# Loading a second weight matrix with converting DMAs issued from GpSimd

## The chip, the cores and the metric

The kernel runs on one core of one Trainium2 chip. The metric is the device time of one execution in microseconds (us), several executions per kernel. TensorE (PE) multiplies (PEld are its weight loads); VectorE (DVE), ScalarE (ACT) and GpSimd (POOL) work elementwise; SyncE (SP) issues DMAs here. The profile books all DMAs, whoever issues them, on the core's 16 DMA engines.

## The reference

Blockwise linear attention, then a two-layer network with SiLU on its output:

```python
# q, k, v: (4, 8, 768, 64) f32
for b in range(nb):                                # blocks of 64 positions
    intra = (q_b @ k_b.T * decay_mask) @ v_b
    inter = (q_b * lam_pow) @ kv_state
    out_b = intra + inter
    kv_state = lam_block * kv_state + (k_b * rev_pow).T @ v_b
x = out as (3072 tokens, 512)
h = x @ w_in                                       # (512, 2048)
g = h * sigmoid(h)
y = g @ w_out                                      # (2048, 512), f32 out
```

w_in and w_out are 4.2 MB each in f32. The kernel multiplies in bf16.

## The kernel before

The tokens go in 24 chunks of 128; the first four form group 0, which runs attention, the up-projection (w_in), then the down-projection (w_out), while the weights still arrive. Both weight matrices come in eight pieces of 512 KB. SP loads each piece as f32 into one of eight buffers; DVE (here and there ACT) casts it to bf16 in its place.

```python
W_IN = [((0, 2), (0, 512)), ((2, 4), (0, 512)), ((0, 4), (512, 768)), ((0, 4), (768, 1024)),
        ((0, 2), (1024, 1536)), ((2, 4), (1024, 1536)), ((0, 2), (1536, 2048)), ((2, 4), (1536, 2048))]
# a row of a piece is 2 KB in DRAM, but 1 KB in pieces 2 and 3

def load_w(which, *pieces):
    for i in pieces:
        src = w_piece(which, i, ...)
        t = wio.tile([128, 1024], F32, name="w_tmp", tag="w_tmp", bufs=WBUFS)      # WBUFS = 8
        ...
        nc.sync.dma_start(out=t, in_=src)
        wtmp[which, i] = t

def cast_w(which, i, e="D"):                       # e: D = DVE, A = ACT
    dst, t = w_piece(...), wtmp.pop((which, i))
    ...                                            # copy t to dst, f32 -> bf16

load_q(0), load_k(0), ..., load_v(3)               # group 0, on the SP queue
load_w("in", *range(8))
load_w("out", *range(6))
load_q(4)
load_k(4), load_k(5)
load_w("out", 6, 7)
load_v(4), load_v(5)
...                                                # the attention of group 0, in the order of ORDER:
#   ... vc:3,D (cast v of chunk 3 on DVE) ... x:1,A ... w:0,DA z:1,o d:3 o:3,att f:0,0 x:3,A w:1,DA kv:3,A f:0,1 ... w:2,D w:3,D
clear_halves(2, 3)                                 # POOL memsets
...
for i in range(4, 8):
    cast_w("in", i)
for m in range(4, 16):
    ffn1(0, m)                                     # up-projection, 4 matmuls of 128x512 each
for i in range(6):
    cast_w("out", i)
down0(0, 2, 3, 0, 1)                               # down-projection: needs w_out pieces 0 and 1
...
```

Of the kernel before, what the change touches and what calls it, by code (L numbers as in the profile page):

```python
# [24 lines left out]
ORDER = """  # L25
# [9 lines left out]
def kernel(  # L35
# [10 lines left out]
    nc = tc.nc  # L46
# [38 lines left out]
        out=ident, in_=ident, compare_op=AL.not_equal, fill=1.0,  # L85
# [5 lines left out]
        out=mask, in_=mask, compare_op=AL.is_ge, fill=0.0,  # L91
# [44 lines left out]
    w_out_bf = wpool.tile([128, KO_OUT, DM], BF16)  # L136
# [7 lines left out]
    def w_piece(which, i, src, dst):  # L144
        (k0, k1), (a, z) = W_IN[i] if which == "in" else ((2 * i, 2 * i + 2), (0, DM))
        return (src if dst is None else dst)[:, k0:k1, a:z]

    def load_w(which, *pieces):
        for i in pieces:
            src = w_piece(which, i, w_in_r if which == "in" else w_out_r, None)  # L150
            t = wio.tile([128, 1024], F32, name="w_tmp", tag="w_tmp", bufs=WBUFS)
            t = t.rearrange("p (ko f) -> p ko f", ko=src.shape[1])
            nc.sync.dma_start(out=t, in_=src)  # L153
            wtmp[which, i] = t

    def move(e, dst, src):
        if e == "A":
            nc.scalar.activation(dst, src, AF.Copy)  # L158
        else:
            nc.vector.tensor_copy(dst, src)  # L160

    def cast_w(which, i, e="D"):

        dst, t = w_piece(which, i, None, w_in_bf if which == "in" else w_out_bf), wtmp.pop((which, i))
        n = dst.shape[1] // len(e)
        for h, x in enumerate(e):
            move(x, dst[:, n * h:n * h + n, :], t[:, n * h:n * h + n, :])
# [27 lines left out]
    def load_q(c):  # L195

        b, blk = divmod(c, NB)
        sl = slice(blk * BLK, (blk + 2) * BLK)
        qf = io.tile([128, H, 2, D], F32, name="qf2", tag="qf2", bufs=2)
        nc.sync.dma_start(out=qf.rearrange("p h r d -> p h (r d)"),  # L200
                          in_=q[b, :, sl, :].rearrange("h (p r) d -> p h (r d)", r=2))
        rawq[c] = qf
# [9 lines left out]
    def load_k(c):  # L212
        rawk[c] = load_1(k, c, "kf", 6)

    def load_v(c):
        vraw[c] = load_1(v, c, "vf", 6)
# [253 lines left out]

    load_q(0), load_k(0), load_k(1), load_q(2), load_k(2), load_v(0), load_k(3), load_v(1), load_v(2), load_v(3)
    load_w("in", *range(8))
    load_w("out", *range(6))
    load_q(4)
    load_k(4), load_k(5)
    load_w("out", 6, 7)
    load_v(4), load_v(5)
    load_c(6)
    load_c(7)
# [20 lines left out]
    def op_z(n, tag="kv"):  # L500
# [8 lines left out]
        "s": keep("s", pe_s), "m": op_m, "d": pe_d, "kv": copy_kv, "o": keep("o", pe_o),  # L509
        "x": lambda c, e: move(e, xt[0][:, :, c * BLK:(c + 1) * BLK], cell["o", c]),  # L510
        "w": lambda i, e: cast_w("in", i, e), "f": op_f, "z": op_z,
    }
    for word in ORDER.split():
        name, _, args = word.partition(":")
        table[name](*[int(a) if a.isdigit() else a for a in args.split(",")])

# [19 lines left out]
# [3 lines that stand above are left out]
        ffn1(0, m)  # L539
    for i in range(6):  # L540
        cast_w("out", i)
# [110 lines left out]
```

## Time and profile before

| | before |
|---|---|
| median of 3 runs | 220.1 us (219.55 to 220.37) |
| span of the profiled run | 218.3 us |
| PE busy | 207.6 us |
| start of group 0's up-projection, second half | 22.48 us |
| start of group 0's down-projection | 35.89 us |

The page of the kernel before: busy time of each engine, with its share of the span and its instructions.

```profile
PE 207.6 (95%) x1642; PEld 129.7 (59%) x1642; DVE 109.8 (50%) x257; ACT 103.9 (48%) x216; POOL 59.7 (27%) x68
```

PE is busy 95% of the span and everything else about half. A change gains or loses only where it moves one of PE's waits, or PE's clock.

The timeline of PE before, in the stretch in question. A line starts with the start and the time taken; in brackets stand PE's idle time before it and what ended it.

```profile
20.18 1.05 PE L419 MATMUL h_ps<-xt,w_in_bf 128*128 128x256 bf16 x8
22.48 13.58 PE L419 MATMUL h_ps<-xt,w_in_bf 128*128 128x256 bf16 x72 [1.25 <-DVE w_in_bf L160]
35.89 7.07 PE L445 MATMUL o_ps<-w_out_bf,g 128*128 128x512 bf16 x32
```

After one wait of 1.25 us for the second w_in piece, PE runs without a break from 22.48 us through the up-projection into the down-projection.

The timeline of DVE before: the cast of the fourth v piece (vpad), then those of the w_in pieces. The bracket of a cast tells that DVE waited for the piece to land.

```profile
18.14 0.42 DVE L160 CAST vpad<-vf 128x512 bf16<-128x512 f32 x1
...
26.20 0.69 DVE L160 CAST w_in_bf<-w_tmp 128x1024 bf16<-128x1024 f32 x1 [0.67 <-DMA w_tmp<-in_moe_w_in_dram]
27.56 0.69 DVE L160 CAST w_in_bf<-w_tmp 128x1024 bf16<-128x1024 f32 x1 [0.66 <-DMA w_tmp<-in_moe_w_in_dram]
28.90 0.69 DVE L160 CAST w_in_bf<-w_tmp 128x1024 bf16<-128x1024 f32 x1 [0.65 <-DMA w_tmp<-in_moe_w_in_dram]
30.27 0.69 DVE L160 CAST w_in_bf<-w_tmp 128x1024 bf16<-128x1024 f32 x1 [0.67 <-DMA w_tmp<-in_moe_w_in_dram]
```

These are pieces 4 to 7. One lands every 1.36 us, which is 385 GB/s: the DMA engines are full (their busy share is 1.04 to 1.05 in every 2 us from 24 to 36 us). Piece 5 serves the last 30 matmuls of the up-projection and piece 7 the last 14. At 0.86 us per four, counted back from 35.89 us, PE needs them at 29.4 and 32.9 us; their casts end at 28.25 (27.56 and 0.69) and 30.96, so the slack is about 1.2 and 1.9 us.

### The profile page before, as it was taken

To read this page: it belongs to the slowest core of one execution; us is meant where nothing else is said; L and a number is where in the kernel's file an instruction comes from. 1 tells how busy PE (TensorE), PEld (TensorE's weight loads), DVE (VectorE), ACT (ScalarE), POOL (GpSimd) and SP (SyncE) were. 2 spreads that over 40 slices of the span, in tenths; PEclk is the share of its full clock that TensorE was granted. 3 is DMA by queue.
4 is the path that set the end of the run, shared out by engine and by line. 5 is a ranking of instruction groups with operands and counts; after the bars stand their busy time and mean duration, and the time that the engine had idled before them with its cause. 6 is when DMAs were issued, how large, how long until landed. Compare 5 with 4: busy or idle time off the path is not lost.

```text
span 218.3 us, 4252 instructions
## 1 busy us (share of the span) xinstructions
PE 207.6 (95%) x1642; PEld 129.7 (59%) x1642; DVE 109.8 (50%) x257; ACT 103.9 (48%) x216; POOL 59.7 (27%) x68
## 2 busy tenths in 40 slices
PE   7778899999899999999989999999999999999994
PEld 2356544456776877766646566556555555566654
DVE  7796455177594668646744553835671333001121
ACT  4776765052662665554554445444444443443310
POOL 7565100616941432333313233433000000000000
PEclk9999999999999999999999999999999999999999
DMA  4999999999997999999999979999610111011112
GB/s 120 243 217 349 378 387 349 248 235 219 237 249 156 200 214 142 228 142 230 216 153 209 204 142 205 223 226 228 128 50 0 48 51 47 2 51 50 48 48 99
DMA packets 97941, 38.04 MB, mean 174 GB/s; under 512 B 86912, under 2 KB 91392, under 8 KB 97920
## 3 DMA queue, kind: packets, MB, share of 16 engines
q1 hardware_dynamic: 97776, 37.76, 80.8%
q8 instruction: 13, 0.21, 0.4%
q14 instruction: 8, 0.07, 0.2%
q10 hardware_dynamic: 144, 0.00, 0.0%
HBM read 27.27 MB, written 6.29 MB: 154 GB/s over the span
## 4 chain that ended last, share of the span: by engine, by line
PE 47%; DMA 30%; SPq 14%; POOL 5%; issue 1%; DVE 1%; POOLq 0%
PE o_ps L445 22%; PE h_ps L419 19%; DMA qf<-in_q_dram 16%; SPq L209 8%; DMA w_tmp<-in_moe_w_in_dram 5%; DMA w_tmp<-in_moe_w_out_dram 5%; POOL qb L245 4%; SPq L263 3%; DMA kn<-kb 2%; PE op L396 2%; SPq L153 2%; DMA kf<-in_k_dram 2%; PE o_part L459 2%; PE sp L365 1%; POOL kb L239 1%
## 5 line engine op out<-in xcount | busy, mean ns | idle before, releaser
L423 ACT ACTIVATE g<-h_ps 128x256 bf16<-128x256 f32 (+2 forms) x144 | 64.8, 455 | 79.9 <-PE h_ps L419 78.6
L419 PE MATMUL h_ps<-xt,w_in_bf 128*128 128x256 bf16 (+2 forms) x592 | 100.1, 304 | 1.8 <-DVE w_in_bf L160 1.3
L445 PE MATMUL o_ps<-w_out_bf,g 128*128 128x512 bf16 x368 | 92.3, 379 | 0.3 <-DVE w_out_bf L160 0.3
L419 PEld LDWEIGHTS <-w_in_bf 128*128 128x128 bf16 x592 | 55.4, 98 | 33.6 <-DVE w_in_bf L160 1.8
L445 PEld LDWEIGHTS <-g 128*128 128x128 bf16 x368 | 34.9, 98 | 30.5 <-issue 0.5
L449 DVE COPY ob<-o_ps 128x512 f32<-128x512 f32 x23 | 15.9, 692 | 43.5 <-PE o_ps L445 43.4
L245 POOL TENSOR_TENSOR qb<-qf,lam_fwd 128x512 bf16<-128x512 f32 x18 | 18.8, 1043 | 63.9 <-DMA qf<-in_q_dram 63.9
L372 DVE TENSOR_TENSOR ss<-sp,mask 128x512 bf16<-128x512 f32 (+1 forms) x48 | 26.2, 585 | 18.1 <-PE sp L365 16.8
L239 POOL TENSOR_TENSOR kb<-kf,lam_bwd 128x512 bf16<-128x512 f32 x23 | 24.3, 1059 | 5.8 <-DMA kf<-in_k_dram 4.9
L276 DVE COPY vpad<-vb 64x256 bf16<-64x256 bf16 x72 | 18.3, 254 | 1.6
L160 DVE CAST kvbd<-kv_ps 64x256 bf16<-64x256 f32 x32 | 13.5, 421 | 9.0 <-PE kv_ps L341 8.8
L404 ACT ACTIVATE xt<-op 128x512 bf16<-128x512 f32 x20 | 11.9, 597 | 9.2 <-PE op L396 8.6
L160 DVE COPY ktbd<-kn 64x512 bf16<-64x512 bf16 x32 | 10.8, 339 | 10.7 <-DMA kn<-kb 10.4
L365 PEld LDWEIGHTS <-ktbd 128*128 128x128 bf16 x192 | 11.2, 98 | 6.9 <-DVE ktbd L160 3.9
L365 PE MATMUL sp<-qt,ktbd 128*128 128x128 bf16 (+1 forms) x192 | 13.4, 210 | 2.0 <-DVE ktbd L160 1.8
L396 PE MATMUL op<-ss,vpad 128*128 128x128 bf16 (+1 forms) x192 | 12.7, 209 | 0.0
L158 ACT ACTIVATE vb<-vf 128x512 bf16<-128x512 f32 x18 | 11.2, 622 | 0.0
L396 PEld LDWEIGHTS <-vpad 128*128 128x128 bf16 x192 | 10.9, 98 | 0.3
L234 POOL TENSOR_TENSOR qb<-qf,lam_fwd 128x512 bf16<-128x512 f32 x4 | 4.6, 1166 | 20.1 <-DMA qf<-in_q_dram 18.5
L504 PE MATMUL warm_ps<-kvbd 128*128 128x512 bf16 x26 | 8.5, 453 | 1.3 <-DVE kvbd L104 1.3
L160 DVE CAST w_in_bf<-w_tmp 128x1024 bf16<-128x1024 f32 (+1 forms) x8 | 5.2, 644 | 6.1 <-DMA w_tmp<-in_moe_w_in_dram 6.1
L341 PEld LDWEIGHTS <-kb 128*128 128x128 bf16 x80 | 6.1, 98 | 3.3 <-issue 0.9
(63 smaller groups left out, 95.4 us busy)
## 6 DMA issues: line engine op xcount, KB each, us to landing
kf<-in_k_dram SPq DMA_DIRECT2D x24, 256.0 KB, 4.8
vf<-in_v_dram SPq DMA_DIRECT2D x24, 256.0 KB, 5.0
out_dram<-ob SPq DMA_DIRECT2D x23, 256.0 KB, 3.7
qf<-in_q_dram SPq DMA_DIRECT2D x18, 256.0 KB, 3.9
w_tmp<-in_moe_w_in_dram SPq DMA_DIRECT2D x8, 512.0 KB, 9.3
w_tmp<-in_moe_w_out_dram SPq DMA_DIRECT2D x8, 512.0 KB, 10.0
qf<-in_q_dram SPq DMA_DIRECT2D x3, 512.0 KB, 5.9
qt<-qb SPq DMA_TRANSPOSE x16, 3.9
```

The lines of the kernel that those rows point to most:

```text
L160: nc.vector.tensor_copy(dst, src)
L209: nc.sync.dma_start(out=t, in_=src[b, :, blk * BLK:(blk + 1) * BLK, :].rearrange("h s d -> s h d"))
L239: VG[e].tensor_tensor(kb, rawk.pop(c).rearrange("s (p j) d -> s p j d", j=2), decay(lam_bwd, c % NB), op=AL.mult)
L245: nc.gpsimd.tensor_tensor(qb, rawq.pop(c).rearrange("s (p j) d -> s p j d", j=2), decay(lam_fwd, c % NB), op=AL.mult)
L276: nc.vector.tensor_copy(vh[64 * j:64 * j + 64, :, h, j, :], vb[64 * h:64 * h + 64, :, j, :])
L365: nc.tensor.matmul(sp[:, p, :], lhsT=lhsT, rhs=qt[:, p, a:], start=True, stop=True)
L372: VG[e].tensor_tensor(ss, sp, m[:, None, :n].to_broadcast([128, 4, n]), op=AL.mult)
L396: nc.tensor.matmul(dst, lhsT=lhsT, rhs=rhs, start=(i == 0), stop=(i >= len(terms) - NP), skip_group_check=True)
L419: nc.tensor.matmul(hp[:, a:z], lhsT=w_in_bf[:, ko, m * 128:(m + 1) * 128], rhs=xt[g][:, ko, a:z], start=(ko == 0 and a == 0), stop=(ko == ...
L423: nc.scalar.activation(gg, hp[:, :n], AF.Silu)
L445: nc.tensor.matmul(o, lhsT=gt[g, ko][:, mt * BLK:(mt + 1) * BLK], rhs=w_out_bf[:, ko, :], start=(ko == 0), stop=(ko == KO_OUT - 1))
L449: nc.vector.tensor_copy(ob, o)
```

## The change

The intent: spare DVE and ACT the w_out casts and SP the w_out issues, by letting DMAs convert on the way. They are issued from GpSimd.

```diff
     def load_w(which, *pieces):
         for i in pieces:
             src = ...
+            if which == "out":
+                nc.gpsimd.dma_start(out=w_piece(which, i, None, w_out_bf), in_=src)
+                continue
 ...
     def cast_w(which, i, e="D"):
+        if which == "out":
+            return
 ...
     load_w("in", *range(8))
-    load_w("out", *range(6))
     load_q(4)
     load_k(4), load_k(5)
-    load_w("out", 6, 7)
 ...
-    for word in ORDER.split():
+    words = ORDER.split()
+    for i, word in enumerate(words):
+        if word == "x:1,A":
+            load_w("out", *range(8))
```

## The prediction

The sum came to 225.5 us (the terms as written add up to 225.6).

> **What bounds the kernel now.** TensorE. The page's busy table gives PE 207.6 of 218.3 us, at full granted clock. By the table of stretches PE is idle 2.6 us in 0-10, 1.4 us in 10-20 and 1.4 us in 20-30; from 30 us on it idles about 2.5 us in all, before the tail. Four matmuls of 128x512 follow each other every 0.86 us (the chain of waits), so they run back to back. DVE is 50% busy, ACT 48%, POOL 27%: what they do costs nothing unless PE waits for it.
>
> **Where the weights are tight.** From 17 to 36 us the DMA engines are full (share about 1.05, 380 to 390 GB/s). All loads are on the one SP queue, in order: w_in, then w_out. In the timeline of DVE the w_in pieces land one per 1.36 us (512 KB): casts start at 23.36, 24.84, 26.20, 27.56, 28.90, 30.27. PE needs them nearly at once: counting 0.86 us per up-projection tile from 22.48 us, the tiles of pieces 4 and 5 start at about 28.5 (last cast ends 28.25) and those of 6 and 7 at about 32.0 (last cast ends 30.96). Slack is 0.3 and 1.0 us. The w_out pieces land with more room (pieces 0 and 1 cast by 33.7, used at 35.9; only a 0.34 us PE wait at 48.5).
>
> **What the change does.** Removes seven DVE casts (0.69 us each) and one ACT cast (1.06 us), all in PE's shadow: worth about 0.3 us. Removes 9.3 us of SP issue, so q, k, v of chunks 4 to 7 are requested earlier: no PE wait worth more than about 1 us hangs on those. Adds eight issues on POOL; behind the last prepared k (ends 15.06 us) nothing holds them, so they start there, not at 21 to 40 us as before. POOL's next urgent work is at 40 us, so issuing may cost it 10 to 20 us unpunished.
>
> **The cost.** The 4 MB of w_out now travel beside w_in instead of after it. [...] At half of 385 GB/s a w_in piece takes 2.7 us instead of 1.36. From about 17 us the last one then lands near 38 (estimate: 8.4 MB at 385 GB/s from 16.5 us) instead of 30.3; its tiles start at about 39 instead of 32. PE loses about 7 us in several waits, mostly before 40 us, and nothing later gives them back. If the cast makes the transfers slower, [...] the loss is 10 us or more[...]. [...]
>
> Sum: 220.1 + 6.5 lost to late w_in - 1 from the gaps that go = 225.5 us. Faster by over 2% would need 4.4 us, more than PE idles after 22.5 us.
>
> **What would show it.** A second, software DMA queue of 4.2 MB read; PE waits on w_in casts between 21 and 40 us of 4 to 8 us in sum; w_in's issue-to-landing median up from 9.3 to 13 us or more; total PE busy about unchanged; PE idle after 45 us at or under before's.
>
> **What would make it wrong.** The software queue gets a small share beside the hardware queue, yet w_out is still on time: then 219 to 221. Or POOL starts the issues later than 15 us. Or cast transfers are far slower than plain ones, or PE's clock falls in the waits: then over 232.

## The result, and the profile after

The changed kernel takes 226.47 us (median of 4 runs, 225.63 to 226.9), against 219.82 us for the kernel before on the same chip. The ratio is 1.029, with a 95% interval of 1.026 to 1.032: slower. All ratios here are the mean time of one kernel's fast runs over that of the other's in the same rounds, so not quite the ratio of the medians. A run counts as slow when it is over 1.5% above the fastest of the same kernel; all runs named are fast unless it is said otherwise. The granted clock is the share of its full clock that TensorE was given, by the profile; 1.00 is full.

The page after, busy time and then DMA queues (packets, MB, share of 16 engines' span):

```profile
PE 209.8 (94%) x1642; PEld 131.2 (59%) x1642; DVE 112.0 (50%) x250; ACT 102.4 (46%) x215; POOL 66.3 (30%) x76
...
q1 hardware_dynamic: 95600, 33.57, 72.1%
q0 software_dynamic: 2176, 2.10, 5.5%
```

The new software queue q0 carries w_out. Its MB are those written as bf16; it reads twice as many.

The timeline of PE after:

```profile
21.23 0.40 PE L346 MATMUL kv_ps<-vpad,kb 128*128 128x128 bf16 x4 [2.18 <-DVE vpad L163]
...
24.18 10.10 PE L424 MATMUL h_ps<-xt,w_in_bf 128*128 128x256 bf16 x50 [1.50 <-DVE w_in_bf L163]
34.99 3.63 PE L424 MATMUL h_ps<-xt,w_in_bf 128*128 128x512 bf16 x16 [0.72 <-DVE w_in_bf L163]
40.45 3.19 PE L424 MATMUL h_ps<-xt,w_in_bf 128*128 128x512 bf16 x14 [1.83 <-DVE w_in_bf L163]
43.48 7.07 PE L450 MATMUL o_ps<-w_out_bf,g 128*128 128x512 bf16 x32
```

Four waits stand where there was one, and the down-projection starts 7.6 us later (43.48 against 35.89). The first two do not wait for late data: the v cast and the first w_in cast, whose data had landed, ended late on DVE. Only 0.72 and 1.83 us are waits for late pieces. The four waits sum to 6.2 us, 5.0 more than before; the other 2.6 us of the delay are, by subtraction, PE at a lower clock (below). The span grew by 5.5 us (223.8 against 218.3), so 2.1 us came back afterwards: from the start of the down-projection on, PE waits 0.6 us in all by the list of waits (2.2 before).

The timeline of DVE after, same casts:

```profile
18.22 2.95 DVE L163 CAST vpad<-vf 128x512 bf16<-128x512 f32 x1
...
31.48 0.69 DVE L163 CAST w_in_bf<-w_tmp 128x1024 bf16<-128x1024 f32 x1 [2.00 <-DMA w_tmp<-in_moe_w_in_dram]
34.24 0.69 DVE L163 CAST w_in_bf<-w_tmp 128x1024 bf16<-128x1024 f32 x1 [2.07 <-DMA w_tmp<-in_moe_w_in_dram]
36.93 0.69 DVE L163 CAST w_in_bf<-w_tmp 128x1024 bf16<-128x1024 f32 x1 [2.00 <-DMA w_tmp<-in_moe_w_in_dram]
39.70 0.69 DVE L163 CAST w_in_bf<-w_tmp 128x1024 bf16<-128x1024 f32 x1 [2.08 <-DMA w_tmp<-in_moe_w_in_dram]
```

Two things are to be seen. The w_in pieces now land 2.7 us apart, twice as far as before, and the last is cast 9.4 us later. And the v cast, the same instruction as before, took 2.95 us instead of 0.42. The timeline of POOL says what it met:

```profile
15.01 5.91 POOL L152 DMA_DIRECT2D w_out_bf<-in_moe_w_out_dram  x8
```

POOL is busy with the eight issues, a median of 0.74 us each, from 15.01 to 20.92 us; DVE's cast ends at 21.17. (The theories below call this descriptor writing; the profile shows the issues and their time, not what they write.) The first w_in cast on DVE was long too, 1.84 us from 22.28 us instead of 0.45. It ran beside two POOL memsets, from 22.00 to 23.83 us, that came later than before because POOL was busy; no run separates this from the issues themselves. The third new thing is in the table of stretches (start and end, then length, busy time of PE, PEld, DVE, ACT, POOL with counts, granted clock, DMA share, GB/s):

```profile
22.00:24.00 2.00, 0.67 (x7) 0.40 (x4) 2.00 (x2) 1.29 (x3) 2.00 (x4) 0.50 1.18 247
24.00:26.00 2.00, 1.82 (x9) 1.33 (x10) 1.97 (x3) 0.46 (x2) 1.94 (x3) 0.50 1.16 247
26.00:28.00 2.00, 2.00 (x12) 1.38 (x11) 0.00 (x0) 0.00 (x0) 0.12 (x1) 0.50 1.18 266
```

PE's granted clock is halved (0.50) from about 22 to 28 us; before it was full throughout (1.00).

### The profile page after: what moved, and what is told of

It reads as the page before. It is cut to its first block, busy times and chain, and to the rows that moved or that the text cites. A ratio compares the mean times of both kernels' runs of the same rounds, so it can differ in the third digit from the quotient of the medians.

```text
span 223.8 us, 4245 instructions
## 1 busy us (share of the span) xinstructions
PE 209.8 (94%) x1642; PEld 131.2 (59%) x1642; DVE 112.0 (50%) x250; ACT 102.4 (46%) x215; POOL 66.3 (30%) x76
## 3 DMA queue, kind: packets, MB, share of 16 engines
q0 software_dynamic: 2176, 2.10, 5.5%
## 4 chain that ended last, share of the span: by engine, by line
PE 69%; ACT 1%; DVE 0%; issue 0%
PE o_ps L450 29%; PE h_ps L424 29%; PE op L401 4%; PE sp L370 3%; PE o_part L464 2%; PE kv_ps L346 1%; ACT xt L409 1%; ACT g L428 0%; DVE ktbd L163 0%; DVE ob L163 0%; PE tp L330 0%; PE tp L328 0%
## 5 line engine op out<-in xcount | busy, mean ns | idle before, releaser
L424 PE MATMUL h_ps<-xt,w_in_bf 128*128 128x256 bf16 (+2 forms) x592 | 102.4, 309 | 4.6 <-DVE w_in_bf L163 4.1
L424 PEld LDWEIGHTS <-w_in_bf 128*128 128x128 bf16 x592 | 56.4, 100 | 37.7 <-DVE w_in_bf L163 5.3
L281 DVE COPY vpad<-vb 64x256 bf16<-64x256 bf16 x72 | 20.6, 286 | 1.6
L409 ACT ACTIVATE xt<-op 128x512 bf16<-128x512 f32 x20 | 11.9, 597 | 11.3 <-PE op L401 10.7
L163 DVE CAST w_in_bf<-w_tmp 128x1024 bf16<-128x1024 f32 (+1 forms) x8 | 7.2, 914 | 11.0 <-DMA w_tmp<-in_moe_w_in_dram 11.0
L163 DVE COPY ktbd<-tk 64x512 bf16<-64x512 bf16 x10 | 4.2, 421 | 12.8 <-PE tk L318 12.3
## 6 DMA issues: line engine op xcount, KB each, us to landing
w_tmp<-in_moe_w_in_dram SPq DMA_DIRECT2D x8, 512.0 KB, 13.7
```

The costliest lines, as they stand in the source:

```text
L163: nc.vector.tensor_copy(dst, src)
L281: nc.vector.tensor_copy(vh[64 * j:64 * j + 64, :, h, j, :], vb[64 * h:64 * h + 64, :, j, :])
L409: nc.scalar.activation(xt[g][:, :, off * BLK:(off + 1) * BLK], op, AF.Copy)
L424: nc.tensor.matmul(hp[:, a:z], lhsT=w_in_bf[:, ko, m * 128:(m + 1) * 128], rhs=xt[g][:, ko, a:z], start=(ko == 0 and a == 0), stop=(ko == ...
```

## The experiments

Two theories were set against each other. A: w_out shares the DMA engines with w_in, and late w_in pieces set the pace. B: writing descriptors on POOL, that is, issuing the DMAs there, blocks DVE's casts, PE waits, and its clock falls. Both were seen in the trace (pieces 2.7 us apart; a cast of 2.95 us and a clock of 0.50); the question was which of them the 6 us are.

| kernel | last w_in cast starts | down-projection starts | median, us | ratio to before (95%) |
|---|---|---|---|---|
| before | 30.27 | 35.89 | 219.82 | 1 |
| the change | 39.70 | 43.48 | 226.47 | 1.029 (1.026 to 1.032) |
| e1: after w_in | 29.51 | 36.84 | 222.43 | 1.011 (1.007 to 1.015) |
| e2: descriptors only | 31.45 | 39.63 | 223.45 | 1.014 (1.011 to 1.018) |
| e3: traffic only | 39.32 | 43.10 | 225.24 | 1.024 (1.020 to 1.028) |
| e4: casts on ACT | 40.92 | 44.71 | 227.00 | 1.032 (1.028 to 1.036) |
| f4: half early | 35.46 | 39.99 | 222.66 | 1.018 (1.013 to 1.023) |
| f6: waits filled | 40.90 | 44.68 | 226.59 | 1.035 (1.031 to 1.039) |
| f3: half late | 29.76 | 35.63 | 219.90 | 1.004 (1.001 to 1.008) |
| f7: quarter late | 29.57 | 35.48 | 221.25 | 1.011 (1.006 to 1.016) |
| f9: half rows | 36.07 | 39.85 | 225.28 (the two fast: 222.69) | none (two of four runs slow) |
| f10: half later | 30.00 | 35.69 | 220.20 | 1.001 (0.995 to 1.007) |

In the five rows where the last w_in cast starts after 36 us (the change, e3, e4, f6, f9), the down-projection starts 3.78 us after it each time, to within 0.01 us: 0.69 us of cast, then the last tiles. There nothing but that piece sets the time. In the kernel before it is 5.62 us: the piece is early by 1.84 us. The change casts it 9.43 us later; less those 1.84 us this is 7.59 us, just what the down-projection lost.

All gave the right result. Times are in us; the columns of starts come from the profiled run of each. The kernel before had medians of 220.27, 219.32 and 219.74 us beside the three sets e1 to e4, f3 to f7 and f9 to f10.

### e1: the eight DMAs held back until w_in is cast

```diff
-        if word == "x:1,A":
-            load_w("out", *range(8))
 ...
     for i in range(4, 8):
         cast_w("in", i)
+    gate = const.tile([128, 1], F32)
+    nc.gpsimd.tensor_copy(gate, w_in_bf[:, 3, 2047:2048])   # waits for the last cast
+    load_w("out", *range(8))
```

> The eight converting DMAs issue only after the last w_in cast (about 31 us), so they meet neither the w_in loads nor the busy stretch of DVE at 15 to 21 us. Theory A (shared DMA bandwidth) and theory B (descriptor generation blocks DVE, then PE's clock falls) both expect the loss gone: down-projection starts at 35.9 to 36.5 us, no PE wait on w_in over 1.5 us, time 218 to 220.5. If the converting DMAs are bad in themselves (slow engines, late w_out), it stays above 222.

The expectation missed: 222.43 us. The timeline of PE:

```profile
36.84 0.60 PE L450 MATMUL o_ps<-w_out_bf,g 128*128 128x512 bf16 x2 [1.13 <-DMA w_out_bf<-in_moe_w_out_dram]
39.02 6.79 PE L450 MATMUL o_ps<-w_out_bf,g 128*128 128x512 bf16 x29 [1.57 <-DMA w_out_bf<-in_moe_w_out_dram]
```

The waits on w_in went back to 1.0 us in all, as both theories say, but w_out itself is now late: issued from 30.89 us on, it isn't there at 35.7. So this run shows that the early start was the harm, and also that w_out has no room to start later as a whole. It doesn't tell A from B.

### e2: the descriptors without the traffic

The kernel before, with eight DMAs of as many rows added on POOL, each of 8 bytes to read (q0 ran 2176 packets in both).

```diff
+    dummy = const.tile([128, KO_OUT, 2], BF16)
     for word in ORDER.split():
+        if word == "x:1,A":
+            for i in range(8):
+                nc.gpsimd.dma_start(out=dummy[:, 2 * i:2 * i + 2, :], in_=w_out_r[:, 2 * i:2 * i + 2, 0:2])
```

> The kernel before, plus eight converting DMAs from GpSimd at 15 us with the same number of descriptors, each of 8 bytes, into a scratch tile: the descriptor cost without the traffic. Theory A alone expects at most 221. Theory B expects DVE's cast of the fourth v piece to take about 3 us instead of 0.4, PE to wait about 2 us at 21 us, perhaps a fall of the granted clock, and 221.5 to 224; if B were the whole cause, 226.

POOL was again busy 5.92 us with the eight issues. From the timeline of DVE:

```profile
18.07 2.95 DVE L160 CAST vpad<-vf 128x512 bf16<-128x512 f32 x1
```

The cast is as long as in the changed kernel, with almost no bytes moved by these DMAs (0.01 MB on q0, 2.10 MB in the change): it is the issuing that blocks it. PE waited 2.2 us for it and 1.9 us for w_in, its clock was halved around 24 to 26 us (the mean clock of all four runs was below that of before, 0.983 to 0.992), and the time rose by 1.4%. So B's mechanism is real and, alone, costs about 3 us (223.45 less 220.27). It is not the whole 6. At the down-projection it is 3.7 us: 2.8 us more waits and, by subtraction, 0.9 us of slow clock. The last w_in cast also came 1.2 us later than before (31.45 against 30.27), but PE came to it later still.

### e3: the traffic without the descriptors

No DMA from POOL: w_in and w_out alternate as f32 on the SP queue, and DVE casts both as they land.

```diff
-WBUFS = 8
+WBUFS = 9
 ...
-    load_w("in", *range(8))
-    load_w("out", *range(6))
+    for i in range(8):
+        load_w("in", i), load_w("out", i)
 ...                                     # w_out casts moved behind the w_in casts they land after
```

> No DMA from GpSimd: w_in and w_out loaded alternately as f32 on the SP queue, w_out cast by DVE as its pieces land: the traffic without the descriptors. Theory A expects a w_in piece per 2.7 us, the last w_in cast near 38 to 40 us, down-projection from 42 to 43.5 us, and 224 to 226.5, although no DVE cast is blocked and PE has no wait at 21 us. Theory B expects about 220.

225.24 us, a ratio of 1.024. In this profile the clock was full from 16 to 44 us and no cast was blocked, yet PE stood 8.0 us for w_in, and the down-projection began at 43.10 us, 0.4 us before that of the change. From the timeline of PE:

```profile
40.07 3.19 PE L419 MATMUL h_ps<-xt,w_in_bf 128*128 128x512 bf16 x14 [1.79 <-DVE w_in_bf L160]
```

The same 14 matmuls start behind the same last piece. (In the other three runs the mean clock was 0.985 to 0.992, and two of them took as long as the profiled one to within 0.2 us.) The traffic alone is enough for nearly all of the delay of the down-projection (7.2 of 7.6 us), and for 5.0 of the 6.65 us in time (225.24 less 220.27). The other 1.7 us are not separated; the intervals of the two ratios overlap. e3 writes f32 and the change bf16, yet pieces 4 to 7 land 2.7 us apart in both. The trace of the change shows the same for single packets: from 30 to 38 us both queues ran 807 packets, nearly all of them rows of 2 KB to read, which took 57.3% of the 16 engines' time on q0 and 56.2% on q1. A converted row of 2 KB held an engine as long as a plain one: the conversion costs the DMA engines nothing that shows, and it saves them nothing.

### e4: the blocked casts moved to ScalarE

```diff
-... vc:3,D ... w:0,DA ... w:1,DA ...
+... vc:3,A ... w:0,A ... w:1,A ...
```

> The changed kernel with the casts that GpSimd's descriptor writing blocked (fourth v piece, w_in pieces 0 and 1) on ScalarE. Theory A: the wait at 21 us goes, but the last w_in pieces still land near 39 us and the time stays at 225 to 227, because the later wait absorbs the earlier one. Theory B: 221 to 223.

227.0 us: taking the block away gained nothing. The wait at 21 us went, and PE stood longer later. The clock fell too, but later, to 0.50 from 38 to 40 us. Why the last piece came 1.2 us later than in the profiled run of the change is open. That run was the fastest of its four, and f6 below, with the same DMAs, has the late time too (40.90), so it may be scatter. The intervals of the two ratios overlap. From the timeline of DVE, w_in pieces 2 to 7:

```profile
26.11 0.69 DVE L163 CAST w_in_bf<-w_tmp 128x1024 bf16<-128x1024 f32 x1 [6.62 <-DMA w_tmp<-in_moe_w_in_dram]
30.32 0.69 DVE L163 CAST w_in_bf<-w_tmp 128x1024 bf16<-128x1024 f32 x1 [3.51 <-DMA w_tmp<-in_moe_w_in_dram]
33.00 0.69 DVE L163 CAST w_in_bf<-w_tmp 128x1024 bf16<-128x1024 f32 x1 [1.99 <-DMA w_tmp<-in_moe_w_in_dram]
35.77 0.69 DVE L163 CAST w_in_bf<-w_tmp 128x1024 bf16<-128x1024 f32 x1 [2.07 <-DMA w_tmp<-in_moe_w_in_dram]
38.45 0.69 DVE L163 CAST w_in_bf<-w_tmp 128x1024 bf16<-128x1024 f32 x1 [1.99 <-DMA w_tmp<-in_moe_w_in_dram]
40.92 0.69 DVE L163 CAST w_in_bf<-w_tmp 128x1024 bf16<-128x1024 f32 x1 [1.77 <-DMA w_tmp<-in_moe_w_in_dram]
```

Piece 3 came 4.2 us after piece 2, the later ones about 2.7 us apart. All are 512 KB. Pieces 2 and 3 are those whose rows are 1 KB; the w_out rows are 2 KB. A reading of the two spacings: if the queues take turns row by row, a 512 KB piece of 1 KB rows travels beside 1 MB of w_out. By an estimate from the rate in the kernel before, 1.5 MB at 385 GB/s, that is 4.1 us. f9 tests that.

### f4: half the dose

w_out pieces 0 to 3 as in the change, 4 to 7 as before.

```diff
-            if which == "out":
+            if which == "out" and i < 4:
                 nc.gpsimd.dma_start(...)
 ...
+    load_w("out", 4, 5)        # on SP, behind w_in; 6 and 7 after k as before
 ...
-            load_w("out", *range(8))
+            load_w("out", *range(4))
```

> Half the dose: w_out pieces 0 to 3 by converting DMAs at 15 us as in the change, 4 to 7 as f32 on the SP queue behind w_in with DVE and ScalarE casts as before. Theory A (w_in shares the DMA engines with whatever w_out is queued early): 2.1 MB less ahead of w_in, so the last w_in cast starts near 35 to 36 us (before 30.3, changed kernel 39.7), down-projection starts near 39.5, time 222 to 223.5. If the loss came from the descriptors or the conversion as such, half of them would give about the same time as e2 or less than 222.

The last w_in cast started at 35.46 us, half way between 30.27 and 39.70 within 0.5 us, and the time was 222.66 us. From the timeline of DVE:

```profile
30.13 0.69 DVE L163 CAST w_in_bf<-w_tmp 128x1024 bf16<-128x1024 f32 x1 [3.29 <-DMA w_tmp<-in_moe_w_in_dram]
31.41 0.69 DVE L163 CAST w_in_bf<-w_tmp 128x1024 bf16<-128x1024 f32 x1 [0.58 <-DMA w_tmp<-in_moe_w_in_dram]
32.76 0.69 DVE L163 CAST w_in_bf<-w_tmp 128x1024 bf16<-128x1024 f32 x1 [0.66 <-DMA w_tmp<-in_moe_w_in_dram]
```

From piece 3 on, when the early half of w_out is through, the spacing is 1.3 to 1.4 us again. The delay follows the bytes that are queued beside w_in.

### f6: PE's waits filled with zero matmuls

A zero matmul (z) multiplies zeros, and nothing reads the result; the kernel before has some already. The edit adds 15 of them (PE has 1657 matmuls, 1642 before), not 16.

```diff
-... w:0,DA z:1,o d:3 ... kv:3,A f:0,1 ...
+... w:0,DA z:10,o d:3 ... kv:3,A z:6,att f:0,1 ...
```

> The changed kernel with 16 more zero matmuls in PE's waits at 19 and 23 us, so that the granted clock does not fall at 22 us. If the slow clock counts, the time falls by 1.5 to 2 us to 224.5. If the late w_in pieces set the pace (theory A), it is absorbed: 225.5 to 226.7, down-projection still from 43 to 43.5 us; the fall may only come later.

226.59 us; the down-projection began at 44.68 us, later than the expected 43 to 43.5. The clock stayed full to 36 us, and only then fell to 0.51 (36 to 38 us), after a wait of 2.07 us. Full clock from 22 to 28 us gained nothing: the down-projection began 3.78 us after the last w_in cast, as in the change. In one of the other three runs the mean clock was 1.000, and it took 226.52 us all the same. So the slow clock of the changed kernel was hidden behind the late pieces. In e2, where no piece comes late enough to hide it, it shows: there the down-projection began 8.2 us after the last w_in cast.

In these runs the length of a single wait does not tell whether the clock falls: it fell to 0.50 or 0.51 after waits of 2.18 us (the change) and 2.07 us (f6), while the profiled run of e3 had waits of 2.09, 2.12 and 1.79 us and kept its clock (1.00). What decides it is not shown by these runs.

### f3, f7 and f10: part of w_out by converting DMAs, held back

These were attempts to keep some of the change's gain. f3: pieces 0 to 3 as before, 4 to 7 by converting DMAs after the last w_in cast. f7: only 6 and 7 so. f10: as f3, but after the cast of w_out piece 3.

```diff
-            if which == "out":
+            if which == "out" and i >= 4:                     # f3 and f10; f7: i >= 6
 ...
+    load_w("out", *range(4))                                  # on SP, behind w_in; f7: range(6)
 ...
+    nc.gpsimd.tensor_copy(gate, w_in_bf[:, 3, 2047:2048])     # f10: w_out_bf[:, 7, DM - 1:DM]
+    load_w("out", *range(4, 8))                               # f7: 6, 7
```

> An attempt to beat both: w_out pieces 0 to 3 as before, 4 to 7 by converting DMAs held back until the last w_in cast. Theory A: w_in as in the kernel before (last cast near 30), no wait on w_out since 4 to 7 are needed only from 43 us on; 218.5 to 220.5. DVE's casts of pieces 0 to 3 may be held up to 3 us by the descriptor writing at 31 to 34 us, which would cost PE 0 to 1 us at 36 us.

> As the last, with only pieces 6 and 7 by converting DMAs after the last w_in cast. They no longer wait on the SP queue for a free buffer and for k, so the 0.3 us wait of PE at 48 us goes; 218.5 to 220, within 1% of the kernel before.

> f3 with the four converting DMAs held back further, until w_out piece 3 is cast (about 35 us). w_in untouched; DVE's casts no longer meet the descriptor writing; k of chunk 5 less starved than in f3 (POOL got it at 43.4). Pieces 4 and 5 are needed at 43 us, 8 us after the issue, so PE may wait up to 1 us. 218.5 to 220.5: within 1% of the kernel before.

219.90, 221.25 and 220.20 us. f3 and f10 are level with the kernel before within 1%, f7 is 1% slower, and none beats it. In f10 PE waited 1.0 us for w_out, as expected. The expectation for f7 missed: its POOL prepared q of chunk 4 from 42.23 us on (40.34 before) and PE waited 1.8 us for it. The load took 13.9 us from issue to landing (11.3 before); that the converting DMAs beside it slowed it is likely, but no run tests it. In f3 DVE's casts of w_out met the descriptor writing and took 0.69 to 0.86 us, far from 2.95; why DVE was held so much less there is not shown.

### f9: e4 with w_out in runs of 1 KB

```diff
-                nc.gpsimd.dma_start(out=w_piece(which, i, None, w_out_bf), in_=src)
+                for h in (slice(0, 256), slice(256, 512)):
+                    nc.gpsimd.dma_start(out=w_piece(which, i, None, w_out_bf)[:, :, h], in_=src[:, :, h])
```

> e4 with each early w_out DMA cut in two by columns, so its reads are runs of 1 KB instead of 2 KB; the bytes are the same, the descriptors double. If an engine takes turns packet by packet, w_in (2 KB rows in all pieces but 2 and 3) now gets two thirds instead of half: pieces 4 to 7 land about 2.0 us apart (e4: 2.7), pieces 2 and 3 about 2.7 apart (e4: 4.2), the last w_in cast near 35 us instead of 40.9, down-projection near 39.5, 222 to 223.5. If the turns go by bytes or time, the spacing stays 2.7 and the time at 227.

From the timeline of DVE, pieces 2 to 7:

```profile
24.53 0.69 DVE L164 CAST w_in_bf<-w_tmp 128x1024 bf16<-128x1024 f32 x1 [5.03 <-DMA w_tmp<-in_moe_w_in_dram]
27.62 0.69 DVE L164 CAST w_in_bf<-w_tmp 128x1024 bf16<-128x1024 f32 x1 [2.40 <-DMA w_tmp<-in_moe_w_in_dram]
29.71 0.69 DVE L164 CAST w_in_bf<-w_tmp 128x1024 bf16<-128x1024 f32 x1 [1.39 <-DMA w_tmp<-in_moe_w_in_dram]
31.83 0.69 DVE L164 CAST w_in_bf<-w_tmp 128x1024 bf16<-128x1024 f32 x1 [1.43 <-DMA w_tmp<-in_moe_w_in_dram]
33.95 0.69 DVE L164 CAST w_in_bf<-w_tmp 128x1024 bf16<-128x1024 f32 x1 [1.43 <-DMA w_tmp<-in_moe_w_in_dram]
36.07 0.69 DVE L164 CAST w_in_bf<-w_tmp 128x1024 bf16<-128x1024 f32 x1 [1.42 <-DMA w_tmp<-in_moe_w_in_dram]
```

The spacing fell from 4.2 to 3.1 us (piece 3) and from 2.7 to 2.1 us (pieces 4 to 7), with the same bytes to move. (For piece 3 equal turns would have given the expected 2.7; the other 0.4 us are not explained.) The packet counts of the change say it directly. The page counts one packet per row: 2176 on q0 in the change, 2048 rows and 128 small ones (4352 in f9, where 128 more packets are under 512 B). From 21 to 25 us, when w_in's 1 KB rows pass, q0 and q1 ran 504 and 506 packets in the change. Each queue got as many rows, so the queue with the longer rows got more bytes. The times scatter: two fast runs of 223.07 and 222.31 us, within what was expected, and two slow ones of 228.93 and 227.49 us; two fast runs give no interval, so only the spacing is used.

One caution: in f9, from the ninth issue on, POOL waited for an earlier DMA of its own to land before it issued the next (2.21 us before the ninth, 0.79 to 1.46 us before the others). That could starve the queue. But from 28 us on it issued 256 KB about every 2.1 us, in which 512 KB of w_in landed: one to two, 256 rows each, as rows of 1 and 2 KB in turn would give.

## Why the prediction was right

The kernel lost 6.65 us; the forecast was 5.4 (225.5 less 220.1). The mechanism was the one forecast: w_out beside w_in halves w_in's rate, and the last w_in piece sets the pace (e3, f4). That the sum came out so close is partly luck, as some of its terms were off in opposite directions.

- *"At half of 385 GB/s a w_in piece takes 2.7 us instead of 1.36."* Right: 2.7 us for the 2 KB pieces. The half was assumed when it was written; it held because the rows of both were 2 KB (807 packets on each queue from 30 to 38 us). For the 1 KB pieces the share was a third (504 and 506 packets from 21 to 25 us; 4.2 us for a piece in e4), which the prediction had not seen. The median time from issue to landing of w_in rose from 9.3 to 13.7 us, as forecast.
- *"The last one then lands near 38 [...]; its tiles start at about 39."* Cast at 39.70, tiles at 40.45 us. *"PE loses about 7 us [...] nothing later gives them back"*: 7.6 us by the start of the down-projection, near, but 2.1 us did come back, where the sum had 1. Loss and return were both about 1 us larger than written. The 7.6 us are also made otherwise than forecast: the piece came 9.4 us later (forecast 7.7), and the slack that took off was 1.8 us (forecast 1.0). And they are not all waits for late pieces: these are 2.55 us in the change. The held casts and the slow clock filled the rest of the time until the last piece came. In e3, without them, PE does wait 8.0 us for w_in.
- *"Nothing holds them, so they start there"*: issued from 15.01 us. *"Issuing may cost it 10 to 20 us"*: it took 5.91.
- *"Removes 9.3 us of SP issue, so q, k, v of chunks 4 to 7 are requested earlier."* Wrong but for one load. In the timeline of SP, q of chunk 4 was issued at 23.75 us instead of 28.95, but the two issues for k of chunks 4 and 5 then took 14.69 us (8.01 before), and q of chunk 6 came at 43.34 us, later than the 41.55 of before. The return of 2.1 us is thus not from earlier requests. PE itself was 7.6 us later, so the waits behind its own later data shrank; that this is the reason was not tested.
- What the issues on POOL do to DVE has no term in the sum. POOL held up DVE, and a cast took seven times as long (2.95 us against 0.42). e2 prices it at about 3 us alone. It didn't show in the sum, because the late w_in pieces came after it and absorbed it (e3 reaches the same point without it; e4, without it, gains nothing).
- *"PE's clock falls in the waits: then over 232."* It fell (to 0.50), without that. It too was absorbed where it lay (f6). *"Total PE busy about unchanged"* was off by 2.2 us for that reason.

So delays that end before the last wait do not simply add: the traffic (e3, about 5 us) and the descriptors with the clock (e2, about 3 us) together gave 6.65 us, 1.5 less than their sum.

## What to carry to other kernels

Before moving a load to another queue, ask what the queue's order was protecting: here the pieces of a single queue landed in the order of issue (one per 1.36 us, w_in before w_out), which kept the second matrix from delaying the first, and losing that cost far more than the spared casts and issues were worth: even where w_in was left alone (f3, f10), sparing half of them gained nothing (1.004, 1.001). In these runs two queues ran as many rows as each other (807 and 807, 504 and 506 packets in the change), so the one with longer rows got more bytes (a w_in piece took 4.2 us with 1 KB rows and 2.7 with 2 KB, beside rows of 2 KB), and a conversion on the way saved no DMA time (807 packets took 57.3% of the engines' time converted and 56.2% plain). When several waits lie in a row, remove them one at a time on the chip: the largest in the trace may be worth nothing while a later one remains (the change's wait of 2.18 us was its longest; e4 removed it and took 227.00 us, not less than 226.47).
